# Half of the pair maxima go through PSUM, and the scores of two blocks lie contiguous there

## The chip, the core and the metric

The kernel runs on one core of a Trainium2 chip. The core has a matrix engine (TensorE, PE in the profile; its weight loads are the row PEld), a vector engine (VectorE, DVE), an activation engine (ScalarE, ACT), a general engine (GpSimd, POOL) and a queue that issues DMAs (SyncE, SP). Each has its own in-order stream of instructions, and they meet only at semaphores. PE writes to PSUM, which has 8 banks of 512 fp32 values per partition; POOL does not use PSUM in this kernel.

The metric is device time in microseconds (us). Three runs of the kernel before took 932.29, 934.55 and 936.86 us; the median is 934.55 us.

## What is computed

The inputs are q, k and v with 8 batches, 8 heads, 576 positions and 64 values per head, and two weight matrices of 512 x 2048 and 2048 x 512. All are fp32. Cut to what matters:

```python
scores = scale * np.matmul(q, k.transpose(0, 1, 3, 2))            # 576 x 576 for each of 64 heads
kth = np.partition(scores, -32, axis=-1)[..., -32:-31]            # the 32nd largest of a row
scores = np.where(scores >= kth, scores, -1e9)
attn = exp(scores - max) / (sum + 1e-9)
x = (attn @ v) as 4608 tokens x 512
h = x @ w_in;  out = np.maximum(h, 0) ** 2 @ w_out                # 4608 x 512
```

The costly step is the 32nd largest of 576 values in each of 36,864 rows.

## The kernel before

**The unit of work** is a task: two row blocks of 128 partitions with 576 scores each. In most tasks the two blocks are the same 128 query rows of two heads (a head pair), so that each head has its 64 values on its own half of the partitions of the transposed q and k (tile `qk`). In the others (`gi == Z`, 16 of 144) they are the last 64 rows of four heads, for two head pairs. There are 144 tasks.

**A task goes through these steps**, by the lines of the profile:

1. `scores` (L505 to L514) or `scores_z` (L516 to L524): PE writes the 2 x 576 fp32 scores to banks 0 to 2 (tile `ss` of pool `ps_s`, a single buffer). The first 512 columns of each block have a bank of their own, the two rests of 64 columns are next to each other in bank 2. The first head's matmuls use the array's rows 0 to 63, the second head's rows 64 to 127. All is one operation of the plan, one after the other on PE.
2. Two copies on ACT bring the scores to SBUF, tile `s`: L533 (1024 columns) and L535 (128 columns).
3. `m`, L589 on DVE: the maximum of each of 288 pairs of a row (column c with column c + 288), for both blocks; one operand is read from PSUM and the other from `s`.
4. `big`, L594 on DVE: the maximum of two pairs, 144 quad maxima per row, to the first quarter of tile `f`, a tensor_reduce.
5. POOL works out the other elements by sums and differences of bit patterns (L586): `t1` = both elements of a pair added, `t2` = both pair maxima added, `mid` = `t2` less `big`, `low` = `t1` less `m`. `f` then holds each row sorted into quad maxima, the lesser pair maxima and the lesser elements.
6. Three rounds on DVE take the largest eight of a prefix of `f` (MAX8, L609) and replace them there (MATCH_REPLACE8, L613); prefixes are 104, 124 and 272 columns long. A last MAX8 over all 576 gives `kth` (L616). The replacing instructions wait for `mid`, the last MAX8 for `low`.
7. ACT makes `w` from `s` and `kth` (L624, twice). PE (`flip`, L644) transposes `s` by nine matmuls and adds nine of `w`, ACT takes the exponential (`p`, L657), PE multiplies with v (`vb,p`), and the sums are divided out.
8. When a chunk of tokens is complete, `feed` runs the two matrix products of the second part (`xt,win` and `wo,g` in the profile), with the square on ACT or POOL.

**The order** is written out by a planner (`Plan.schedule`, L120) before the kernel runs. Every operation has an engine, an assumed duration, a priority (a due time `tg` = 12 + 6 n for task n, with an offset) and the tiles that it takes. The planner plays the five streams against each other by the assumed durations, and whenever an engine is free, it gives it the ready operation of the lowest due time. The outcome is one fixed stream per engine; on the chip an instruction that is late holds up all behind it. A tile is given out again once all operations that use it have ended. For the score operation the planner assumes 1.25 us.

Of the kernel before, what the change touches and what calls it, by code (L numbers as in the profile page):

```python
# [5 lines left out]
ALU = mybir.AluOpType  # L6
ACTF = mybir.ActivationFunctionType
AX = mybir.AxisListType
# [283 lines left out]
def bass_top_k_attn__then__act_relu_squared_kernel(  # L292
# [8 lines left out]
    NB, H, S, D = q.shape  # L301
    assert H == 8 and S == 576 and D == 64, (NB, H, S, D)
    HALF, QUART = S // 2, S // 4
    NHP = 4
    NPAIR = NB * NHP
    NBLK = 9
# [12 lines left out]
    T0 = 12.0  # L319
    LEAD = 20  # L320
    ME = 10
    MQ = 0
    MP = 3
    LAG = 20
    STEP = 3.2
    LATE = 1.5
# [39 lines left out]
    ps32 = nc.alloc_psum_tensor("ps", [P, 8, 512], FP32)  # L366
    ps16 = ps32[:, :, :].bitcast(BF16)

    ps_s, ps_e, psum = Pool("ps_s", 1), Pool("ps_e", 1), Pool("psum", 2)
    BASE = {"ps_s": 0, "ps_e": 3, "psum": 6}  # L370

    def tile(nm):
        return Tile(pools[nm])

    def at(t):
        return mem[t.pool.name][t.slot]
# [7 lines left out]
    def wide(t):  # L384

        b = BASE[t.pool.name]
        return ps32[:, b:b + 3, :].rearrange("p b c -> p (b c)")[:, 0:2 * S]

    em = Emitter(nc)
    act, vec, gp, pe = nc.scalar, nc.vector, nc.gpsimd, nc.tensor  # L390
# [3 lines left out]
    Z = 4  # L394
# [26 lines left out]
    def two(ap, step, n_):  # L421

        return bass.AP(ap.tensor, ap.offset, [ap.ap[0], [step, 2], [1, n_]])
# [9 lines left out]
    def build(full, weights, pl):  # L433
# [7 lines left out]
        def load_pair(b, hp, base):  # L441
            rq, rk, rv = tile("rq"), tile("rk"), tile("rv")

            def load(t, src, queue=nc.sync):
                def fn():
                    r = at(t)
                    res = [queue.dma_start(r[:, 0:4, h, :], src[b, 2 * hp + h, 0:512, :].rearrange(
                        "(tb p) d -> p tb d", p=P)) for h in range(2)]
                    res.append(queue.dma_start(
                        r[0:64, 4, :, :], src[b, 2 * hp:2 * hp + 2, 512:576, :].rearrange("h p d -> p h d")))  # L450
                    return res
                return fn

            def loadv():
                r = at(rv)
                res = [nc.sync.dma_start(r[:, 4 * h:4 * h + 4, :], v[b, 2 * hp + h, 0:512, :].rearrange(
                    "(tb p) d -> p tb d", p=P)) for h in range(2)]

                for h, low, e in ((0, 0, 8), (1, 64, 9), (1, 0, 10) if hp % 2 == 0 else (0, 64, 11)):
                    res.append(nc.sync.dma_start(r[low:low + 64, e, :], v[b, 2 * hp + h, 512:576, :]))  # L460
                return res

            pl.op("sp", 2.3, base - 80, load(rq, q), w=[rq], take=[rq], sem=slot_sem, ndma=3)
            via = "act" if not full and not state["pairs"] else None
            state["pairs"] += 1
            pl.op("sp", 2.3, base - 79.9, load(rk, k, nc.scalar if via else nc.sync), w=[rk], take=[rk], sem=slot_sem,
                  ndma=3, via=via)
            pl.op("sp", 2.3, base - 70, loadv, w=[rv], take=[rv], sem=slot_sem, ndma=5)
            qk, vb = tile("qk"), tile("vb")
            tq, tk, tx = Tile(psum), Tile(psum), Tile(psum)  # L470

            def t4(o, src):
# [12 lines left out]
            pl.op("pe", .48, base - 44.9, t4(tk, rk), r=[rk], w=[tk], take=[tk], order=[o_q])  # L485
            pl.op("pe", .3, base - 44.8, t5, r=[rq, rk], w=[tx], take=[tx], order=[o_q])
            pl.op("act", .6, base - 42.5, lambda: act.copy(at(qk)[:, 0, 0:512], bank(tq)), r=[tq], w=[qk])
            pl.op("act", .6, base - 42.4, lambda: act.copy(at(qk)[:, 1, 0:512], bank(tk)), r=[tk], w=[qk])  # L488
            pl.op("act", .3, base - 42.3, lambda: act.copy(
                at(qk)[:, :, 512:576], bank(tx)[:, 0:128].rearrange("p (a c) -> p a c", a=2)), r=[tx], w=[qk])  # L490
            pl.op("gp", .8, base + 5, lambda: gp.tensor_copy(at(vb)[:, :, 0:D], at(rv)[:, :, :]),
                  r=[rv], w=[vb], take=[vb])
            return qk, vb

        def top_k(gi, qks, tg):

            n = state["n"]
            state["n"] += 1
            ss, st = Tile(ps_s), tile("s")

            def scores():
                o = wide(ss)
                for h, to, c0, n_ in ((0, 1024, 512, 64), (0, 0, 0, 512), (1, 512, 0, 512), (1, 1088, 512, 64)):  # L505
                    x = at(qks[h])
                    if to == 1088:
                        pe.wait_ge(fence, fences[0])
                    ins = mm(o[:, to:to + n_], x[64 * h:64 * h + 64, 0, 128 * gi:128 * gi + 128],
                             x[64 * h:64 * h + 64, 1, c0:c0 + n_], to != 1088)  # L510
                    if to == 1024:
                        fences[0] += 1
                        ins.then_inc(fence, 1)
                return ins  # L514

            def scores_z():  # L516
                o = wide(ss)
                for i in range(2):
                    x = at(qks[i])
                    for to, c0, n_, first in ((1024 + 64 * i, 512, 64, i == 0), (512 * i, 0, 512, True)):  # L520
                        for h in range(2):
                            ins = mm(o[64 * h:64 * h + 64, to:to + n_], x[64 * h:64 * h + 64, 0, 512:576],
                                     x[64 * h:64 * h + 64, 1, c0:c0 + n_], first)
                return ins  # L524

            qu = sorted(set(qks), key=lambda t: t.num)
            pl.op("pe", 1.25 if gi != Z else 1.4, tg - LEAD, scores if gi != Z else scores_z, r=qu, w=[ss], take=[ss, st])


            def flat():  # L530
                return at(st)[:, :, :].rearrange("p i c -> p (i c)")

            cp = [pl.op("act", 1.1, tg - LEAD + 1, lambda: act.copy(  # L533
                two(flat(), 640, 512), two(wide(ss), 512, 512)), r=[ss], w=[st]),
                pl.op("act", .35, tg - LEAD + 1, lambda: act.copy(  # L535
                    flat()[:, 512:640], wide(ss)[:, 1024:1152]), r=[ss], w=[st])]

            dk = [0]

            def dve(dur, fn, dp=0, **kw):  # L540
                dk[0] += 1
                return pl.op("dve", dur, tg + .33 * dk[0] + dp, fn, **kw)
# [11 lines left out]
            f = tile("f")  # L554
            prev = [[], []]
            if full:
                a, sh = tile("a"), tile("sh")
                for rnd in range(4):
                    src = st if rnd == 0 else f
                    for i in range(2):  # L560
                        get = dict(r=[st]) if rnd == 0 else dict(hold=[f])
                        if rnd == 3:
# [4 lines left out]
                                       after=prev[i], take=[a] if rnd == 0 and i == 0 else [],  # L567
                                       w=[a] if rnd == 0 else [], **(
                                           get if rnd == 0 else dict(hold=[f, a])))]
# [11 lines left out]
            else:  # L581

                m, t1, t2 = tile("m"), tile("t1"), tile("t2")

                def whole(dur, prio, op, o, x, y, **kw):
                    return pl.op("gp", dur, prio, lambda: gp.tensor_tensor(  # L586
                        o().bitcast(I32), x().bitcast(I32), y().bitcast(I32), op), **kw)

                dve(.67, lambda: vec.tensor_tensor(  # L589
                    at(m)[:, :, :], two(wide(ss), 736, HALF), two(flat()[:, HALF:], HALF, HALF), ALU.max),  # L590
                    dp=-ME, r=[ss], hold=[st], after=cp, w=[m], take=[m])
                whole(1.38, tg, ALU.add, lambda: at(t1)[:, :, :], lambda: at(st)[:, :, 0:HALF],
                      lambda: at(st)[:, :, HALF:S], r=[st], w=[t1], take=[t1])
                big = dve(.67, lambda: vec.tensor_reduce(  # L594
                    at(f)[:, :, 0:QUART], at(m)[:, :, :].rearrange("p i (a c) -> p i c a", a=2), AX.X, ALU.max),
                    dp=-MQ, r=[m], w=[f], take=[f])
                whole(.77, tg - MP, ALU.add, lambda: at(t2)[:, :, :], lambda: at(m)[:, :, 0:QUART],
                      lambda: at(m)[:, :, QUART:HALF], r=[m], w=[t2], take=[t2])
                mid = whole(.77, tg - MP, ALU.subtract, lambda: at(f)[:, :, QUART:HALF], lambda: at(t2)[:, :, :],
# [1 line left out]
                low = whole(1.38, tg + 2, ALU.subtract, lambda: at(f)[:, :, HALF:S], lambda: at(t1)[:, :, :],  # L601
                            lambda: at(m)[:, :, :], r=[t1, m], w=[f])
# [373 lines left out]
```

## Time and profile before

| | |
|---|---|
| median of three runs | 934.55 us |
| the profiled execution | 930.32 us |
| its span, first to last instruction | 928.2 us |
| DVE busy | 864.2 us |
| PE busy | 810.1 us |
| POOL busy | 750.3 us |
| ACT busy | 742.8 us |
| mean granted clock of PE | 0.985 |

The profiled execution is 0.45% under the median of the runs; 2.1 us of it lie outside its span. Busy time is the union of an engine's instructions: two that overlap count once. Matmuls are pipelined, and each is shown until its result has left the array, so that the distance between the starts of two matmuls, not the duration of one, is the time that it takes from PE.

### The profile page before, as it was taken

Reading aid. Unit: us, or ns where it says so; the run is one execution under the profiler, and the core shown is the slowest. Engines: PE = TensorE matmul, PEld = TensorE weight load, DVE = VectorE, ACT = ScalarE, POOL = GpSimd, SP = SyncE. Lnnn points to the kernel's source line nnn. Section 1 sums busy time; section 2 is a strip of 40 time slices with the busy share of each in tenths; the row PEclk is TensorE's granted clock in tenths of the full one; section 3 lists DMA queues with packets and bytes.
Section 4 is the critical chain, followed back from the end, with each engine's and each line's share of the span. In section 5 each row is a group of like instructions: output and inputs, shape, how many; then the busy total and the mean of one; then the engine's idle time right before and its main releaser. Section 6 shows DMA issues by size and latency. Waiting matters only on the chain.

```text
span 928.2 us, 20946 instructions
## 1 busy us (share of the span) xinstructions
PE 810.1 (87%) x7253; PEld 565.7 (61%) x7330; DVE 864.2 (93%) x3269; ACT 742.8 (80%) x1277; POOL 750.3 (81%) x794
## 2 busy tenths in 40 slices
PE   5766889997689999888888898888998999999996
PEld 4555567766465666656566666656666655665664
DVE  3999999999999999999999999999999999998931
ACT  3665898987699878997799977998779789787762
POOL 6998988878777888777877887877899986899961
PEclk9898999999899999999999999999999999999999
DMA  6742521034101222111210131111211010000101
GB/s 138 190 129 91 141 54 53 14 88 91 39 6 37 53 51 63 27 29 49 58 45 16 40 89 37 41 39 39 52 38 26 13 37 13 24 13 1 43 27 38
DMA packets 126978, 48.11 MB, mean 52 GB/s; under 512 B 119184, under 2 KB 119184, under 8 KB 126864
## 3 DMA queue, kind: packets, MB, share of 16 engines
q1 hardware_dynamic: 125664, 46.39, 19.8%
q8 instruction: 59, 0.97, 0.4%
q14 instruction: 55, 0.45, 0.2%
q10 hardware_dynamic: 1200, 0.30, 0.2%
HBM read 37.22 MB, written 9.44 MB: 50 GB/s over the span
## 4 chain that ended last, share of the span: by engine, by line
DVE 45%; PE 35%; ACT 14%; issue 3%; DMA 1%; POOL 1%; SPq 0%; DVEq 0%
PE ps L428 27%; DVE f L613 13%; DVE kth L616 10%; DVE c L609 10%; PE ps L431 9%; DVE m L589 6%; DVE f L594 5%; ACT p L657 5%; ACT w L624 3%; ACT s L533 2%; ACT g L737 1%; ACT g L751 1%; DMA rq<-in_q_dram 1%; ACT xt L711 0%; ACT qk L488 0%
## 5 line engine op out<-in xcount | busy, mean ns | idle before, releaser
L613 DVE MATCH_REPLACE8 f<-c,f 128x104 f32<-128x104 f32 (+2 forms) x864 | 267.2, 317 | 0.4 <-issue 0.3
L609 DVE MAX8 c<-f 128x8 f32<-128x104 f32 (+2 forms) x864 | 243.7, 321 | 0.1
L428 PE MATMUL ps<-qk 64*128 64x64 f32 (+3 forms) x1280 | 213.9, 454 | 32.8 <-DVE m L589 31.6
L624 ACT ACTIVATE w<-s,kth 128x576 bf16<-128x576 f32 x288 | 222.3, 782 | 6.2 <-DVE kth L616 6.1
L586 POOL TENSOR_TENSOR t<-s 128x576 int32<-128x576 int32 x144 | 203.1, 1413 | 17.7 <-ACT s L535 17.6
L431 PE MATMUL ps<-ident,s 128*128 128x128 f32 x1296 | 200.2, 283 | 16.0 <-ACT w L624 15.4
L533 ACT COPY s<-ps 128x1024 f32<-128x1024 f32 x144 | 146.5, 1017 | 84.2 <-PE ps L428 83.8
L616 DVE MAX8 kth<-f 128x8 f32<-128x576 f32 x288 | 203.4, 748 | 1.6 <-POOL f L586 1.6
L586 POOL TENSOR_TENSOR f<-t,f 128x288 int32<-128x288 int32 x144 | 114.4, 795 | 110.8 <-DVE f L594 94.7
L586 POOL TENSOR_TENSOR f<-t,m 128x576 int32<-128x576 int32 x144 | 202.7, 1408 | 0.0
L428 PEld LDWEIGHTS ps<-qk 64*128 64x128 f32 (+1 forms) x1280 | 129.2, 180 | 110.2 <-DVE m L589 48.1
L657 ACT ACTIVATE p<-ps 128x1152 bf16<-128x1152 f32 x144 | 162.9, 1131 | 33.5 <-PE ps L428 32.6
L431 PEld LDWEIGHTS ps<-ident,s 128*128 128x128 f32 x1296 | 147.0, 143 | 50.1 <-ACT w L624 21.1
L428 PE MATMUL ps<-xt,win 128*128 128x512 bf16 (+3 forms) x674 | 126.8, 324 | 13.7 <-ACT g L737 7.4
L428 PE MATMUL ps<-wo,g 128*128 128x512 bf16 x529 | 134.2, 379 | 4.5 <-ACT xt L711 1.2
L589 DVE TENSOR_TENSOR m<-ps,s 128x576 f32<-128x576 f32 x144 | 107.5, 747 | 19.3 <-ACT s L535 16.9
L428 PE MATMUL ps<-steep_bf,w 128*128 128x128 bf16 x1296 | 121.4, 221 | 0.0
L586 POOL TENSOR_TENSOR t<-m 128x288 int32<-128x288 int32 x144 | 115.1, 799 | 0.0
L594 DVE TENSOR_REDUCE f<-m 128x288 f32<-128x576 f32 x144 | 106.7, 747 | 0.1
L737 ACT ACTIVATE g<-ps 128x512 bf16<-128x512 f32 (+1 forms) x152 | 87.2, 581 | 20.2 <-PE ps L428 19.7
L428 PEld LDWEIGHTS ps<-steep_bf,w 128*128 128x128 bf16 x1296 | 98.4, 99 | 3.6
L428 PEld LDWEIGHTS ps<-xt,win 128*128 128x128 bf16 x704 | 57.7, 98 | 51.8 <-ACT g L737 11.8
(57 smaller groups left out, 774.6 us busy)
## 6 DMA issues: line engine op xcount, KB each, us to landing
rq<-in_q_dram SPq DMA_DIRECT2D x64, 128.0 KB, 2.5
rv<-in_v_dram SPq DMA_DIRECT2D x64, 128.0 KB, 2.4
rk<-in_k_dram SPq DMA_DIRECT2D x62, 128.0 KB, 2.6
out_dram<-o SPq DMA_DIRECT2D x31, 256.0 KB, 2.1
g<-in_moe_w_in_dram SPq DMA_DIRECT2D x8, 512.0 KB, 4.7
g<-in_moe_w_out_dram SPq DMA_DIRECT2D x8, 512.0 KB, 3.9
rv<-in_v_dram SPq DMA_DIRECT2D x96, 16.0 KB, 2.2
out_dram<-o SPq DMA_DIRECT2D x10, 128.0 KB, 2.4
```

Source lines behind the costliest of these rows:

```text
L428: return pe.matmul(o, l, r, start=start, stop=stop, skip_group_check=True)
L431: return pe.matmul(o, i, ident, is_transpose=True, skip_group_check=True, **kw)
L533: cp = [pl.op("act", 1.1, tg - LEAD + 1, lambda: act.copy(two(flat(), 640, 512), two(wide(ss), 512, 512)), r=[ss], w=[st]), pl.op("act", . ...
L586: return pl.op("gp", dur, prio, lambda: gp.tensor_tensor(o().bitcast(I32), x().bitcast(I32), y().bitcast(I32), op), **kw)
L589: dve(.67, lambda: vec.tensor_tensor(at(m)[:, :, :], two(wide(ss), 736, HALF), two(flat()[:, HALF:], HALF, HALF), ALU.max), dp=-ME, r=[ss] ...
L594: big = dve(.67, lambda: vec.tensor_reduce(at(f)[:, :, 0:QUART], at(m)[:, :, :].rearrange("p i (a c) -> p i c a", a=2), AX.X, ALU.max), dp ...
L609: lambda i=i, t=t, c0=c0, c1=c1: vec.max(eighth(t, i), at(f)[:, i, c0:c1]),
L613: lambda i=i, t=t, c0=c0, c1=c1: vec.match_replace(at(f)[:, i, c0:c1], eighth(t, i), at(f)[:, i, c0:c1], NEG), hold=[f])]
L616: ks.append(chain(kth, i, prev[i] + [low], .665, lambda i=i: vec.max(eighth(kth, i), at(f)[:, i, :]), hold=[f]))
L624: pl.op("act", .77, tw + .8 * i, lambda i=i: act.activation(at(wt)[:, i, :], at(st)[:, i, :], ACTF.Relu, bias=kth[:, i, n:n + 1], scale=-1.0),
L657: pl.op("act", 1.15, tt + 1, lambda: act.activation(at(pt)[:, :, :].rearrange("p k q -> p (k q)"), wide(e), ACTF.Exp, scale=0.125), r=[e], ...
L737: return act.activation(at(g)[:, 0:kf * nt], bank(hh)[:, 0:kf * nt], ACTF.Relu)
```

## The change

Three things are changed together.

*Where the scores lie.* The 2 x 576 scores are now contiguous over banks 0 to 2 (1152 columns), and one ACT copy of 1152 columns takes the place of the two copies.

*Two score operations in place of one.* `scores(0)` makes the first head's block (64 + 512 columns, banks 0 and 1), `scores(1)` the second head's (128 + 448 columns, banks 2 and 1). For the Z tasks, `scores_z(0)` and `scores_z(1)` are divided by head pair. The second one writes to bank 2, whose columns 128 to 415 are a new single-buffer tile `sq` of pool `ps_q`, and it takes this tile; so it waits until the previous user is through with it. The planner is told 0.2 and 1.05 us for them (0.65 and 0.75 for Z).

*The pair maxima in two halves.* `m1` is the upper half of the pair maxima (2 x 144), which DVE now writes to PSUM (`sq`); `m0` is the lower half, which goes to SBUF tile `m` as before. A new ACT copy `mc` brings `m1` to its place in `m`, since POOL needs it there. `big` is now a tensor_tensor maximum of `m0` in SBUF with `m1` in PSUM, 2 x 144 outputs, and waits for `m0` and for `mc`. Its due time is 6 us earlier (`MQ` 0 to 6).

The order of the last 64 positions of the second head is rotated, so v is loaded with shifted rows (`64 * h`); number and size of the DMAs stay.

```diff
@@ pools
+    ps_s, ps_q, ps_e, psum = Pool("ps_s", 1), Pool("ps_q", 1), Pool("ps_e", 1), Pool("psum", 2)
+    BASE = {"ps_s": 0, "ps_q": 2, "ps_e": 3, "psum": 6}
-    MQ = 0
+    MQ = 6
+    MA = 12
+    M1 = 1
@@ top_k
-                for h, to, c0, n_ in ((0, 1024, 512, 64), (0, 0, 0, 512), (1, 512, 0, 512), (1, 1088, 512, 64)):
+            def scores(h):
+                o, x = wide(ss), at(qks[h])
+                for to, c0, n_ in ((512, 512, 64), (0, 0, 512)) if h == 0 else ((1024, 448, 128), (576, 0, 448)):
...
-            pl.op("pe", 1.25 if gi != Z else 1.4, tg - LEAD, scores if gi != Z else scores_z, r=qu, w=[ss], take=[ss, st])
+            fn = scores if gi != Z else scores_z
+            sc = pl.op("pe", .2 if gi != Z else .65, tg - LEAD, lambda: fn(0), r=[qks[0]], w=[ss], take=[ss, st])
+            sc = pl.op("pe", 1.05 if gi != Z else .75, tg - LEAD, lambda: fn(1), r=[qks[1]], w=[ss] + ([sq] if M1 else []),
+                       take=[sq] if M1 else [], after=[sc])
-            cp = [pl.op("act", 1.1, tg - LEAD + 1, lambda: act.copy(
-                two(flat(), 640, 512), two(wide(ss), 512, 512)), r=[ss], w=[st]),
-                pl.op("act", .35, tg - LEAD + 1, lambda: act.copy(
-                    flat()[:, 512:640], wide(ss)[:, 1024:1152]), r=[ss], w=[st])]
+            cp = [pl.op("act", 1.2, tg - LEAD + 1, lambda: act.copy(
+                at(st)[:, :, :].rearrange("p i c -> p (i c)"), wide(ss)), r=[ss], w=[st])]
...
-                dve(.67, lambda: vec.tensor_tensor(
-                    at(m)[:, :, :], two(wide(ss), 736, HALF), two(flat()[:, HALF:], HALF, HALF), ALU.max),
-                    dp=-ME, r=[ss], hold=[st], after=cp, w=[m], take=[m])
+                    m1 = dve(.36, lambda: vec.tensor_tensor(quarter(), *parts(QUART, QUART), ALU.max), dp=-ME,
+                             r=[ss], hold=[st, sq], after=cp)
+                    m0 = dve(.36, lambda: vec.tensor_tensor(at(m)[:, :, 0:QUART], *parts(0, QUART), ALU.max), dp=-ME,
+                             r=[ss], hold=[st], after=cp, w=[m], take=[m])
+                    mc = pl.op("act", .45, tg - MA, lambda: act.copy(at(m)[:, :, QUART:HALF], quarter()), hold=[sq],
+                               w=[m], after=[m1, m0])
+                    big = dve(.36, lambda: vec.tensor_tensor(
+                        at(f)[:, :, 0:QUART], at(m)[:, :, 0:QUART], quarter(), ALU.max), dp=-MQ,
+                        hold=[m, sq], after=[m0, mc], w=[f], take=[f])
...
-                big = dve(.67, lambda: vec.tensor_reduce(
-                    at(f)[:, :, 0:QUART], at(m)[:, :, :].rearrange("p i (a c) -> p i c a", a=2), AX.X, ALU.max),
-                    dp=-MQ, r=[m], w=[f], take=[f])
```

More of the change, by code (lines that the diff above doesn't have):

```diff
@@ L303, in bass_top_k_attn__then__act_relu_squared_kernel @@
     HALF, QUART = S // 2, S // 4
+    REST = (512, 0)
     NHP = 4
@@ L367, in bass_top_k_attn__then__act_relu_squared_kernel @@
     ps16 = ps32[:, :, :].bitcast(BF16)
-    ps_s, ps_e, psum = Pool("ps_s", 1), Pool("ps_e", 1), Pool("psum", 2)
-    BASE = {"ps_s": 0, "ps_e": 3, "psum": 6}
+    ps_s, ps_q, ps_e, psum = Pool("ps_s", 1), Pool("ps_q", 1), Pool("ps_e", 1), Pool("psum", 2)
+    BASE = {"ps_s": 0, "ps_q": 2, "ps_e": 3, "psum": 6}
     def tile(nm):
@@ L455, in loadv @@
                 r = at(rv)
-                res = [nc.sync.dma_start(r[:, 4 * h:4 * h + 4, :], v[b, 2 * hp + h, 0:512, :].rearrange(
+                res = [nc.sync.dma_start(r[:, 4 * h:4 * h + 4, :], v[b, 2 * hp + h, 64 * h:64 * h + 512, :].rearrange(
                     "(tb p) d -> p tb d", p=P)) for h in range(2)]
                 for h, low, e in ((0, 0, 8), (1, 64, 9), (1, 0, 10) if hp % 2 == 0 else (0, 64, 11)):
-                    res.append(nc.sync.dma_start(r[low:low + 64, e, :], v[b, 2 * hp + h, 512:576, :]))
+                    res.append(nc.sync.dma_start(r[low:low + 64, e, :], v[b, 2 * hp + h, REST[h]:REST[h] + 64, :]))
                 return res
@@ L498, in top_k @@
             state["n"] += 1
-            ss, st = Tile(ps_s), tile("s")
-            def scores():
-                o = wide(ss)
-                for h, to, c0, n_ in ((0, 1024, 512, 64), (0, 0, 0, 512), (1, 512, 0, 512), (1, 1088, 512, 64)):
-                    x = at(qks[h])
-                    if to == 1088:
+            ss, st, sq = Tile(ps_s), tile("s"), Tile(ps_q)
+            def scores(h):
+                o, x = wide(ss), at(qks[h])
+                for to, c0, n_ in ((512, 512, 64), (0, 0, 512)) if h == 0 else ((1024, 448, 128), (576, 0, 448)):
+                    if to == 576:
                         pe.wait_ge(fence, fences[0])
                     ins = mm(o[:, to:to + n_], x[64 * h:64 * h + 64, 0, 128 * gi:128 * gi + 128],
-                             x[64 * h:64 * h + 64, 1, c0:c0 + n_], to != 1088)
-                    if to == 1024:
+                             x[64 * h:64 * h + 64, 1, c0:c0 + n_], to != 576)
+                    if to == 512:
                         fences[0] += 1
@@ L514, in scores, with scores_z @@
                 return ins
[L516 to L521, printed above, removed]
+            def scores_z(i):
+                o, x = wide(ss), at(qks[i])
+                if i == 0:
+                    runs = [((512, 512, 64), (0, 0, 512)), ((512, 0, 64), (0, 64, 512))]
+                else:
+                    runs = [((1024, 384, 128), (576, 512, 64), (640, 0, 384)), ((1024, 448, 128), (576, 0, 448))]
+                for k_ in range(3):
+                    for h in range(2):
+                        if k_ < len(runs[h]):
+                            to, c0, n_ = runs[h][k_]
                             ins = mm(o[64 * h:64 * h + 64, to:to + n_], x[64 * h:64 * h + 64, 0, 512:576],
-                                     x[64 * h:64 * h + 64, 1, c0:c0 + n_], first)
+                                     x[64 * h:64 * h + 64, 1, c0:c0 + n_], not 576 <= to < 1024)
                 return ins
-            qu = sorted(set(qks), key=lambda t: t.num)
-            pl.op("pe", 1.25 if gi != Z else 1.4, tg - LEAD, scores if gi != Z else scores_z, r=qu, w=[ss], take=[ss, st])
-            def flat():
-                return at(st)[:, :, :].rearrange("p i c -> p (i c)")
-            cp = [pl.op("act", 1.1, tg - LEAD + 1, lambda: act.copy(
-                two(flat(), 640, 512), two(wide(ss), 512, 512)), r=[ss], w=[st]),
-                pl.op("act", .35, tg - LEAD + 1, lambda: act.copy(
-                    flat()[:, 512:640], wide(ss)[:, 1024:1152]), r=[ss], w=[st])]
+            fn = scores if gi != Z else scores_z
[4 more added lines that the diff above has]
+                at(st)[:, :, :].rearrange("p i c -> p (i c)"), wide(ss)), r=[ss], w=[st])]
             dk = [0]
@@ L587, in whole, with parts, quarter @@
                         o().bitcast(I32), x().bitcast(I32), y().bitcast(I32), op), **kw)
-                dve(.67, lambda: vec.tensor_tensor(
-                    at(m)[:, :, :], two(wide(ss), 736, HALF), two(flat()[:, HALF:], HALF, HALF), ALU.max),
-                    dp=-ME, r=[ss], hold=[st], after=cp, w=[m], take=[m])
+                def parts(a, n_):
+                    return two(wide(ss)[:, a:], S, n_), at(st)[:, :, HALF + a:HALF + a + n_]
+                def quarter():
+                    return two(ps32[:, 2, 128:416], QUART, QUART)
+                if M1:
+                    m1 = dve(.36, lambda: vec.tensor_tensor(quarter(), *parts(QUART, QUART), ALU.max), dp=-ME,
[7 more added lines that the diff above has]
+                        hold=[m, sq], after=[m0, mc], w=[f], take=[f])
+                else:
+                    dve(.67, lambda: vec.tensor_tensor(at(m)[:, :, :], *parts(0, HALF), ALU.max), dp=-ME,
+                        r=[ss], hold=[st], after=cp, w=[m], take=[m])
+                    big = dve(.67, lambda: vec.tensor_reduce(
+                        at(f)[:, :, 0:QUART], at(m)[:, :, :].rearrange("p i (a c) -> p i c a", a=2), AX.X, ALU.max),
+                        dp=-MQ, r=[m], w=[f], take=[f])
                 whole(1.38, tg, ALU.add, lambda: at(t1)[:, :, :], lambda: at(st)[:, :, 0:HALF],
                       lambda: at(st)[:, :, HALF:S], r=[st], w=[t1], take=[t1])
-                big = dve(.67, lambda: vec.tensor_reduce(
-                    at(f)[:, :, 0:QUART], at(m)[:, :, :].rearrange("p i (a c) -> p i c a", a=2), AX.X, ALU.max),
-                    dp=-MQ, r=[m], w=[f], take=[f])
                 whole(.77, tg - MP, ALU.add, lambda: at(t2)[:, :, :], lambda: at(m)[:, :, 0:QUART],
```

## The prediction

> **What bounds the kernel now.** I read the shares of busy time first, then the same by stage, then what DVE and PE wait for, then single rows of the timeline for prices. By stage (the windows view; span, busy time of each engine with its instructions, granted PE clock, DMA share, GB/s):
>
> ```profile
> 0.00:100.00 100.00, 66.89 (x532) 51.40 (x534) 82.63 (x311) 60.11 (x97) 85.63 (x112) 0.91 0.55 138
> 100.00:850.00 750.00, 674.51 (x6143) 470.37 (x6209) 740.59 (x2803) 639.84 (x1101) 615.31 (x627) 1.00 0.17 42
> 850.00:928.00 78.00, 68.74 (x581) 43.94 (x588) 40.99 (x157) 42.81 (x80) 49.32 (x57) 0.98 0.10 32
> ```
>
> The order is PE, PEld, DVE, ACT, POOL. From 100 to 850 us DVE is busy 740.6 of 750: it is the bound, at about 5.95 us per task. The last 78 us belong to PE. The waits of DVE in the middle stage are small, and those of PE are waits for DVE:
>
> ```profile
> DVE f L613 <- POOL f L586: 6.1, 7, 1.9
> DVE m L589 <- ACT s L535: 1.9, 4, 0.8
> ...
> PE ps L428 <- DVE m L589: 27.4, 43, 2.8
> ```
>
> DVE never waits long for scores: the loop from `m` by way of scores and copies to the next `m` has room. What the change touches is priced from these groups (busy us, mean ns of one) and these PE rows (start, length):
>
> ```profile
> L533 ACT COPY s<-ps 128x1024 f32<-128x1024 f32 x144 | 146.5, 1017 | 84.2 <-PE ps L428 83.8
> L535 ACT COPY s<-ps 128x128 f32<-128x128 f32 x144 | 40.7, 282 | 0.0
> L589 DVE TENSOR_TENSOR m<-ps,s 128x576 f32<-128x576 f32 x144 | 107.5, 747 | 19.3 <-ACT s L535 16.9 <-POOL f L586 2.0
> L594 DVE TENSOR_REDUCE f<-m 128x288 f32<-128x576 f32 x144 | 106.7, 747 | 0.1
> L609 DVE MAX8 c<-f 128x8 f32<-128x272 f32 x288 | 112.6, 431 | 0.0
> ```
> ```profile
> 505.56 0.59 PE L428 MATMUL ps<-xt,win 128*128 128x512 bf16 x2
> 506.09 1.34 PE L428 MATMUL ps<-qk 64*128 64x64 f32 x8
> 507.37 0.29 PE L431 MATMUL ps<-ident_bf,x 128*128 128x128 bf16 x2
> ...
> 511.02 2.17 PE L428 MATMUL ps<-qk 64*64 64x64 f32 x16 [0.15 <-DVE m L589]
> 513.12 0.36 PE L428 MATMUL ps<-vb,p 128*128 128x65 bf16 x6
> ```
>
> **How full PE really is.** Its busy time counts pipeline tails, so I take starts. A score operation holds PE from 506.09 to 507.37, 1.28 us (the median over all is 1.278). It starts 0.53 us after a pair of 512-column matmuls whose own steps are 0.216 each (0.59 less 0.379 for one, as a group has it), so the change from full-array to half-array matmuls costs 0.09 on the way in; between other kinds the trace has no such gap. By starts: scores 128 x 1.28 + 16 x 2.10 + 144 x 0.09 = 210 us; transposes of s and matmuls of w 1296 x (0.109 + 0.056) = 214; the second part 2 x 576 x 0.216 = 249; v 47, q and k 31, x 8. Sum 759 us, 82% of the span. The same steps on the matmuls that start from 100 to 850 us give 632 us, 84%. Where PE was fullest, in 150 to 200, 750 to 800 and 850 to 900 us, it reached 93, 95 and 92%.
>
> **The change part by part.**
>
> *DVE.* `m` and `big` go, three instructions of half the length come. Durations overlap, so I use starts again: in the timeline a 576-column instruction is followed after 0.66 us (600 ns at 0.96 columns per ns, and 65 ns). 288 columns then take 0.365. Per task 3 x 0.365 = 1.10 for 1.33: 0.23 us less, 33 us over 144 tasks. No row has DVE writing to PSUM; `m` (reads PSUM) and `big` (does not) are both 747 ns, so PSUM as a source costs nothing visible. The upper bound is no overlap at all, 0.45 each by the 272-column MAX8 (0.431): 1.35, no gain. I take 0.23, since every DVE pair without a wait shows the overlap; an end below it has nothing for it.
>
> The Trainium skill speaks against cutting here: "VectorE: DVE Perf Modes", in its section on the fixed extra latency of SBUF-source instructions, advises tiles of at least 512 elements, and gives (N + 151)/0.96 ns for an fp32 tensor_tensor. By that, an estimate, the saving would be 2 x 757 less 3 x 457 = 143 ns per task, 21 us in all. The 747 ns rows agree with the formula as a duration, but not as a distance between starts.
>
> *ACT.* Removed: 146.5 + 40.7 = 187.2 us. Added: one copy of 1152 columns, 1.12 us by the slope between 128 and 1024 columns (the exponential of 1152 takes 1.131), 162 us; and `mc`, 288 columns, about 0.40 between the copies of 260 (382 ns) and 512 (583 ns). That is 58 us, with 0.38 and 0.58 as ends. ACT goes from 743 to 776 us; in the middle stage from 640 to about 669 of 750. Not the bound. `mc` waits for DVE, and behind it in ACT's stream stand `p` and `w`.
>
> *PE.* The columns stay, but not their company. The 1.28 us hold only because the two heads use different rows of the array: each head alone is two passes of 512 at 0.425 and two short ones, and the passes of the heads run in pairs. In the changed streams the second half waits for the previous `big`, and the planner has filled the time between: of 128 normal tasks 112 have other matmuls between the halves, of 16 Z tasks 14. What a half costs alone is to be read from the Z row: it is two successive operations of 576 columns, all row groups alike, 511.02 to 513.12: 2.10 us, 1.05 each. Apart, each half has the change of shape to itself: 0.09 in, and about 0.10 out (the last 512-column pass of a Z task is followed after 0.520, against 0.425 inside). 2.10 + 0.19 - 1.28 = 1.01 us more; added up by single passes it is 0.92. I take 0.95. For a Z task only 0.19 is new. In the middle stage some 102 such tasks lie: 97 + 3 = 100 us more, 632 to 732 of the present 750 us: **98%**. DVE asks for 741 less 126 x 0.23 = 712. PE takes over as the bound.
>
> *Waits.* New: `scores(1)` on PE waits for `big`, and what stands behind it are the transposes, v products and second-part matmuls of a PE that has no time to lose; `big` on DVE waits for `mc`, with the next MAX8 behind it; between `m0` and `big` stand two MAX8 of 576 (1.33 us), which cover 0.40 plus one more ACT copy, not `p` (1.13) and `w` (0.78) together. Gone: `f` for POOL's `mid`, 6 us in the middle, as `big` now runs one task ahead; I leave these in PE's shadow. POOL's work and the DMAs stay the same; SP is asked for no more.
>
> *Sum.* PE at 94%, between the mean (93) and the best of its three fullest stretches: 732/0.94 = 779 us for the middle stage, 29 more. At the start DVE saves 3 us and PE loses about as much: 0. In the last stage, already PE's, three tasks' scores: +3. The profiled execution of 930.3 us becomes 962. The runs' median lies 4 us above that execution, so I predict 965.
>
> **The rivals.**
>
> *A, PE is the bound with the usual holes* (the sum): at 95 and 92% the middle takes 771 and 796, which gives 958 and 983; with a few us for the first stage, 950 to 985. Chance 0.60.
>
> *B, faster: DVE stays the bound.* It ends on the other side, if the halves apart cost what they cost together; then the 33 us are all gained and the run takes about 900. It decides at PE's need: below 712 us in the middle stage. That asks for under 0.75 us per split task and no holes at all, or for the second half to overlap with what is put between, of which I see nothing, as those matmuls use all rows. Even a full PE leaves 732. Chance 0.07, with 900 to 929.
>
> *C, it comes out even:* the planner's order happens to keep PE at 97 to 98%, which no stretch of 50 us reached. 930 to 939, chance 0.10.
>
> *D, the loop becomes the bound.* From `m0` on: half (1.15 with both changes), the matmuls between (mean 1.07 by starts, over 1.5 in three tasks of ten), half (1.15), copy 1.12, `m1` and `m0` 0.73, and some 0.5 of latencies: 5.7 us on average, 6.2 and more where much stands between; a queue on ACT comes on top. If this is paid in every second task with 1 us, the middle stage becomes 126 x 6.5 = 819 us: about 1007. The present DVE waits (1.9 us for the copy) say nothing against it, as the present loop is 2 us shorter. Chance 0.23, 985 to 1015.
>
> **How the numbers follow.** A and D together are 0.83 for slower; 0.5% of the time, 4.7 us, is about what a measurement can tell from no change. Faster is B, 0.07; the same is C, 0.10. The range leaves out B, nearly all of C and the end of D: 938 to 1002. The unknown price of PSUM writes (up to 33 us on DVE) fits in it: under A DVE has 779 less 712 us to spare in the middle stage.
>
> **What the profile after should show.** DVE busy about 833 us, its share down to 87%, with waits for the one copy of `s` where it had none; the time of `qk` matmuls up from 214 to over 300 us; PE busy at 95% or more in the middle; three DVE instructions of about 0.45 us; the copy at 1.12 and `mc` at 0.4. If DVE stays at 98% and PE has holes, B is right and my price of a split half is wrong. If PE has over 10% holes and DVE waits at `m1`, it is D. If the granted clock falls with a fuller PE, all is later than I say.

## The result, and the profile after

The changed kernel takes 1032.6 us (four runs, 1026.8 to 1037.2) against 933.4 us for the kernel before beside it. The ratio is 1.106, with a 95% interval from 1.099 to 1.112: 10.6% slower, where 3.3% had been forecast and the range ended at 1002 us. The profiled execution took 1032.64 us with a span of 1030.8.

By stage (windows view of the changed kernel; span, busy time of PE, PEld, DVE, ACT, POOL, granted PE clock, DMA share, GB/s):

```profile
0.00:100.00 100.00, 85.10 (x469) 52.43 (x470) 69.03 (x279) 56.24 (x84) 73.66 (x100) 0.91 0.46 114
100.00:850.00 750.00, 728.28 (x5653) 442.56 (x5650) 663.04 (x2708) 611.56 (x985) 570.50 (x574) 0.99 0.18 44
850.00:950.00 100.00, 99.42 (x672) 53.98 (x672) 68.45 (x276) 75.60 (x131) 63.14 (x69) 1.00 0.05 15
950.00:1031.00 81.00, 71.53 (x575) 43.00 (x573) 38.60 (x152) 42.89 (x78) 47.29 (x54) 0.98 0.10 31
```

From 100 to 850 us PE is now busy 728 of 750, and DVE, which had 741, has 663. The page's chain of work that ended last says the same; in the kernel before, DVE held 45% of it and PE 35%:

```profile
PE 82%; ACT 8%; DVE 7%; issue 2%; POOL 1%; DMA 0%; SPq 0%
```

The granted clock of PE explains little of the loss: it is 0.980 on average against 0.985, which is some 5 us of the span (an estimate).

DVE's waits turn to the copy of the scores (engine, line, whom it waited for, us in total, times, longest):

```profile
DVE ps L601 <- ACT s L538: 124.0, 109, 14.9
DVE rzall L706 <- ACT av L704: 22.1, 7, 10.4
DVE f L607 <- ACT m L605: 16.7, 32, 3.5
```

PE itself hardly waits for the maxima: 14 us in all for `big` (L607) and `m0` (L603), where in the kernel before it waited 31.6 us for `m`.

```profile
PE ps L431 <- DVE f L607: 8.4, 12, 1.2
PE ps L431 <- DVE m L603: 5.8, 15, 1.0
```

The groups show that the new instructions cost about what was said: three DVE instructions of 0.44 to 0.47 us, one copy of 1.12 us, `mc` of 0.40 us.

```profile
L538 ACT COPY s<-ps 128x1152 f32<-128x1152 f32 x144 | 161.2, 1120 | 76.0 <-PE ps L431 72.1 <-PE ps L434 1.9
L601 DVE TENSOR_TENSOR ps<-ps,s 128x288 f32<-128x288 f32 x144 | 66.9, 465 | 125.4 <-ACT s L538 124.0
L607 DVE TENSOR_TENSOR f<-m,ps 128x288 f32<-128x288 f32 x144 | 63.6, 442 | 17.2 <-ACT m L605 16.7
L605 ACT COPY m<-ps 128x288 f32<-128x288 f32 x144 | 58.2, 404 | 6.8 <-DVE m L603 6.7
```

What was dearer than forecast is the split score operation. These are PE's rows around one task in the timeline (start, length):

```profile
505.33 1.35 PE L431 MATMUL ps<-qk 64*128 64x64 f32 x4
506.61 0.66 PE L434 MATMUL ps<-ident,rk 128*128 128x128 f32 x4
507.10 1.03 PE L431 MATMUL ps<-wo,g 128*128 128x512 bf16 x4
508.06 1.24 PE L431 MATMUL ps<-qk 64*128 64x128 f32 x4
509.23 0.81 PE L431 MATMUL ps<-vb,p 128*128 128x65 bf16 x20
```

The first half holds PE from 505.33 to 506.61 (1.28 us), the second from 508.06 to 509.23 (1.17 us), each with 0.09 us before it for the change of shape: 2.63 us, against 1.28 + 0.09 before. Added up by starts, scores take 376 us of PE instead of 210 (the prediction's sum). All of PE's work by starts is about 928 us, more than the 839 us that DVE is busy. Apart from the scores it is unchanged.

Two theories were tested. **S**: the price of the split on PE sets the time. **L**: the new wait of the second half for `big`, through the shared bank 2, makes the loop from task to task too long, and PE is busy only because it is late.

### The profile page after: what moved, and what is told of

The parts are those of the page before. It is cut to its first block, busy times and chain, and to the rows that moved or that the text cites. A ratio compares the mean times of both kernels' runs of the same rounds, so it can differ in the third digit from the quotient of the medians.

```text
span 1030.8 us, 21271 instructions
## 1 busy us (share of the span) xinstructions
PE 984.3 (95%) x7362; PEld 592.0 (57%) x7362; DVE 839.1 (81%) x3413; ACT 786.3 (76%) x1277; POOL 754.6 (73%) x794
## 4 chain that ended last, share of the span: by engine, by line
PE 82%; ACT 8%; DVE 7%; issue 2%; POOL 1%; DMA 0%; SPq 0%
PE ps L431 64%; PE ps L434 18%; ACT s L538 3%; DVE f L634 2%; ACT p L678 2%; DVE c L630 1%; DVE kth L637 1%; ACT w L645 1%; DVE m L603 1%; DVE ps L601 1%; ACT g L758 1%; DVE f L607 0%; POOL t L589 0%; DMA rq<-in_q_dram 0%; ACT xt L732 0%
## 5 line engine op out<-in xcount | busy, mean ns | idle before, releaser
L431 PE MATMUL ps<-qk 64*128 64x64 f32 (+8 forms) x1312 | 384.3, 445 | 16.6 <-DVE f L607 8.4
L538 ACT COPY s<-ps 128x1152 f32<-128x1152 f32 x144 | 161.2, 1120 | 76.0 <-PE ps L431 72.1
L637 DVE MAX8 kth<-f 128x8 f32<-128x576 f32 x288 | 205.5, 747 | 1.9 <-POOL f L589 1.9
L434 PE MATMUL ps<-ident,s 128*128 128x128 f32 x1296 | 203.9, 286 | 3.2 <-ACT w L645 1.9
L431 PEld LDWEIGHTS ps<-qk 64*128 64x128 f32 (+1 forms) x1312 | 150.9, 180 | 89.8 <-DVE f L634 23.0
L601 DVE TENSOR_TENSOR ps<-ps,s 128x288 f32<-128x288 f32 x144 | 66.9, 465 | 125.4 <-ACT s L538 124.0
L431 PE MATMUL ps<-wo,g 128*128 128x512 bf16 x576 | 144.3, 380 | 0.4 <-ACT g L758 0.4
L431 PE MATMUL ps<-xt,win 128*128 128x512 bf16 (+3 forms) x704 | 133.8, 328 | 7.5 <-ACT g L758 3.0
L431 PEld LDWEIGHTS ps<-wo,g 128*128 128x128 bf16 x576 | 49.7, 98 | 66.5 <-issue 17.9
```

What stands on the lines that cost most here:

```text
L431: return pe.matmul(o, l, r, start=start, stop=stop, skip_group_check=True)
L434: return pe.matmul(o, i, ident, is_transpose=True, skip_group_check=True, **kw)
L538: cp = [pl.op("act", 1.2, tg - LEAD + 1, lambda: act.copy(at(st)[:, :, :].rearrange("p i c -> p (i c)"), wide(ss)), r=[ss], w=[st])]
L601: m1 = dve(.36, lambda: vec.tensor_tensor(quarter(), *parts(QUART, QUART), ALU.max), dp=-ME, r=[ss], hold=[st, sq], after=cp)
L637: ks.append(chain(kth, i, prev[i] + [low], .665, lambda i=i: vec.max(eighth(kth, i), at(f)[:, i, :]), hold=[f]))
```

## The experiments

**1. The scores joined again, everything else as changed.**

```diff
-            sc = pl.op("pe", .2 ..., lambda: fn(0), ..., take=[ss, st])
-            sc = pl.op("pe", 1.05 ..., lambda: fn(1), ..., take=[sq], after=[sc])
+            pl.op("pe", 1.25 if gi != Z else 1.4, tg - LEAD, lambda: [fn(0), fn(1)][1], r=qu,
+                  w=[ss, sq], take=[ss, st, sq])
```

> Edit: the changed kernel, with both halves of the scores in one PE operation again (so they run side by side in the array); it takes the quarter of bank 2 as a whole, so all scores of a task now wait for the previous `big`. Everything else as changed. Theory S (a split half is dear on PE: in the trace after, 1.28 and 1.17 us and twice 0.09 for the change of shape, 2.63 us against 1.37 before, for all 128 normal tasks): score time on PE falls from 376 us (by starts) to about 220, PE is no longer full, and DVE with its 33 us less becomes the bound again: 895 to 930 us. Rival L (the new wait for `big` and the longer loop cost the time): the wait now holds back the whole score operation, so the loop is longer still: 1000 us or more, DVE waiting for the copy of `s` in most tasks.

941.9 us, ratio to the kernel before 1.010 (1.008 to 1.013). So 91 of the 99 us went with the split, though all scores now wait for `big`. S has its main point, L's 1000 us are out. The expected 895 to 930 were missed too: DVE has 709 us of work in the middle stage, and waits. One score operation in this layout takes 1.44 us (median), not 1.28.

```profile
DVE ps L601 <- ACT s L538: 32.7, 36, 12.6
DVE f L634 <- POOL f L589: 20.2, 19, 2.4
...
DVE f L607 <- ACT m L605: 12.3, 15, 2.5
```

**2. The kernel before, with the two heads one after the other.**

```diff
-                    if to == 1088:
+                    if to in (512, 1088):
                         pe.wait_ge(fence, fences[0])
...
-                    if to == 1024:
+                    if to in (1024, 0):
                         fences[0] += 1
                         ins.then_inc(fence, 1)
```

> Edit: the kernel before, with one thing added: inside the score operation the second head's matmuls wait until the first head's have ended. Streams, layout, maxima and planner are as before. Theory S: the two halves one after the other take 2.58 us where they took 1.28 side by side (so the trace after shows it where they stand together): 128 x 1.3 = 166 us more for PE, 917 of need; PE about 94% full in the middle stage: 631 + 110 x 1.3 = 774, over 0.94 gives 823 us there, 990 to 1025 in all, PE busy 95%, DVE with waits for the copy of `s`. Rival L (wait for `big`, bank 2, loop): none of it is here, and DVE has its old work: 930 to 950 us.

1112.5 us, ratio 1.193: more than S said. The score operation takes 2.63 us (median) where it took 1.28, and nothing else was touched:

```profile
500.04 2.69 PE L428 MATMUL ps<-qk 64*128 64x64 f32 x8
502.66 0.66 PE L431 MATMUL ps<-ident,s 128*128 128x128 f32 x4
```

The direction is S's, and the 930 to 950 us that L gave for the old maxima are out. But here the whole 2.63 us also stand between `m` and the copy, and DVE waited 138 us for the copy; so this run is a price of lost company and of a longer loop together. PE's granted clock was low as well (0.94 on average, down to 0.5 in a stretch near 100 us), so part of the excess may be that.

**3. `big` from SBUF alone, in the kernel before.** It asks whether the way through PSUM is needed.

```diff
-                big = dve(.67, lambda: vec.tensor_reduce(
-                    at(f)[:, :, 0:QUART], at(m)[:, :, :].rearrange("p i (a c) -> p i c a", a=2), AX.X, ALU.max),
+                big = dve(.36, lambda: vec.tensor_tensor(
+                    at(f)[:, :, 0:QUART], at(m)[:, :, 0:QUART], at(m)[:, :, QUART:HALF], ALU.max),
```

> Edit: the kernel before, with one line changed: `big` is a tensor_tensor maximum of the two halves of `m`, both in SBUF (2 x 144 outputs), in place of the tensor_reduce over 2 x 288. No PSUM, no split. If an SBUF source costs DVE no more than a PSUM source: 0.365 for 0.66 us by starts, 144 x 0.30 = 43 us less on DVE, the bound; with PE at 751 us of need, 885 to 905 us. If two SBUF operands get in the way of POOL, or the other way round (the reason there might be for the way through PSUM): `big` or POOL's instructions get longer, over 0.5 us for `big` or over 0.83 for POOL's 288-column ones, and the time is 920 us or more.

939.3 us, ratio 1.005 (1.001 to 1.008). The second alternative came true: with both operands in SBUF the same maximum takes 631 ns, with one in PSUM 442 (L607 above). DVE's busy time falls by 17 us and not by 43.

```profile
L594 DVE TENSOR_TENSOR f<-m 128x288 f32<-128x288 f32 x144 | 89.0, 631 | 0.2
```

POOL's instructions are hardly longer (0.82 us for 0.795 in the 288-column `mid`). The mean of 631 ns hides two cases, which the trace tells apart. 90 of the 144 maxima take under 0.49 us, and 84 of these start while POOL runs nothing. The other 54 take 0.53 to 1.7 us: every one starts while a POOL instruction runs, and ends 0.31 us after that instruction has ended. In the changed kernel, with one operand in PSUM, 97 of the 144 start while POOL runs, and none takes more than 0.46 us. So with both operands in SBUF the maximum waits for POOL's instruction to end. One of the 54:

```profile
434.72 1.40 POOL L586 TENSOR_TENSOR f<-t,m 128x576 int32<-128x576 int32 x1
434.81 1.62 DVE L594 TENSOR_TENSOR f<-m 128x288 f32<-128x288 f32 x1
```

**4. The layout alone**: scores joined, `m` and `big` as before (`M1 = 0`, `MQ = 0`), so that only the contiguous scores and the one copy are left.

> Edit: the changed kernel with both halves of the scores in one operation and with the maxima as before (`m` whole, in SBUF, `big` a tensor_reduce, due time of `big` as before). What is left of the change is the contiguous scores and the one copy. Theory S: PE and DVE have the work of the kernel before, ACT 26 us less, which is not the bound: 925 to 938 us. Rival L has nothing to add, as nothing waits for `big`: the same. If it is over 950, the layout itself (a bank that both heads write) costs PE time, and neither theory is whole.

943.9 us, ratio 1.010 (1.006 to 1.015). The layout costs 1% by itself, a little over the expected interval: its score operation takes 1.44 us. In the old order one head begins with its long matmuls and the other with its short one; in the new one both begin with the short ones. There the kernel has the second head's 448 columns wait for the first head's short matmuls (both write to bank 1): in the trace of experiment 1 they start 0.26 us after the matmul of the same head before them, against 0.11 in a half alone. That is 0.15 of the 0.16 us. Between experiments 4 and 1 the maxima through PSUM change nothing in the time.

**5. PE spared elsewhere**: the changed kernel without the mask matmuls.

```diff
-                for o, c, start in outs:
-                    ins = mm(o, wf[:, c:c + 128], minus[:, :], False)
```

> Edit: the changed kernel without the nine matmuls of `w` in every task (the mask is left out, so that all keys count in the softmax); everything waits for `w` as it did. PE is spared 1296 x 0.056 = 73 us. Theory S (PE, full with 928 us of need by starts, sets the time): the time falls by about as much, 950 to 970 us. Rival L (the loop from `big` over the scores to the next `big` sets it, PE being busy only because it is late): the loop is as long as before, 1015 us or more.

1014.7 us, 18 us less, at the edge of what L expected (1015 or more) and far from S's. By progress (the end of `kth` of a task in the trace), tasks 48 to 128 take 6.23 us each, against 6.58 in the changed kernel: 0.35 of the 0.50 us spared. But the 16th task ended at 142 us instead of 129. The granted clock was 0.80 in the first 100 us and 0.87 in the next 200; a second execution had a mean clock of 0.966 for 0.946 and took as long. PE's waits for `big` and `m0` are 15.5 us in all here, so the loop does not account for the missing time either. The clock may account for part of it (106 us at half clock against 37 in the changed kernel, about 34 us of PE's time, an estimate), but the second execution speaks against its being all. This run left the question open.

**6. `big` ahead of `mc`**, in the joined kernel of experiment 1: the loop without the two MAX8 of 576.

```diff
-                    big = dve(.36, ..., dp=-MQ, hold=[m, sq], after=[m0, mc], w=[f], take=[f])
+                    big = dve(.36, ..., dp=-ME, hold=[m, sq], after=[m1, m0], w=[f], take=[f])
-                    mc = pl.op("act", .45, ..., hold=[sq], w=[m], after=[m1, m0])
+                    mc = pl.op("act", .45, ..., hold=[sq], w=[m], after=[big])
```

> Edit: the run with the joined scores (942 us, DVE 832 us busy but waiting for the copy of `s`, for `mc` and for POOL), with `big` ahead of `mc`: it follows `m0` at once and waits for nothing on ACT, and `mc` waits for `big`. The loop from one score operation to the next loses the two MAX8 of 576 between `m0` and `big` (1.33 us) and gains `mc` (0.4 and a queue on ACT). If the loop is what kept the joined run from the 33 us that DVE was spared: 905 to 930 us. If it is the longer score operation (1.44 for 1.28 us) and PE's queue: 938 to 945, as before.

945.7 us, ratio 1.015 (1.009 to 1.022): no gain. PE now waits for `mc` (33 us) in place of `big` (35 us).

**7. The same maxima in the old layout**, with `big` ahead of `mc` and the two copies kept.

> Edit: the kernel before, with its layout, its two copies and its one score operation (1.28 us), and only the maxima changed: `m1` to PSUM (bank 2, columns 128 to 415), `m0`, `big` at once after them, then `mc`. Against the run with the same order in the contiguous layout it spares PE 0.16 us per normal task (20 us in all) and costs ACT 26 us. DVE is spared 30 us. If DVE's work counts: 895 to 920. If one engine less full does not help since the loop is longer by the wait for `mc`: 930 or more.

938.8 us, ratio 1.006 (1.002 to 1.011). DVE is busy 828 us for 864, and a task takes 5.88 us in the steady part for 5.99; the last task ends 12 us earlier than before. The end after it takes 44 us for 29.

**8. True durations for the planner**, in the changed kernel: 1.3 and 1.2 us for the halves.

```diff
-            sc = pl.op("pe", .2 if gi != Z else .65, ...
-            sc = pl.op("pe", 1.05 if gi != Z else .75, ...
+            sc = pl.op("pe", 1.3 if gi != Z else 1.15, ...
+            sc = pl.op("pe", 1.2 if gi != Z else 1.15, ...
```

> Edit: the changed kernel with the durations that the halves had on the chip told to the planner (1.3 and 1.2 us for 0.2 and 1.05; 1.15 each for Z): only the order of the streams changes, no work. If PE's need alone sets the time: 1020 to 1045, as the changed kernel. If the wrong durations put PE's work in an order that makes it and the others wait: 20 us less or more, 1010 and below.

1009.3 us, ratio 1.082 (1.072 to 1.093). The work is the same and PE's need by starts is 928 us in both, but 23 us are gained by the order. The clock has a small part in that at most: the second run, with a mean clock of 0.985, took 1012.9 us, and two runs of the changed kernel with 0.982 and 0.987 took 1032.5 and 1037.2. In the steady stage PE has almost no idle time left:

```profile
300.00:850.00 550.00, 547.33 (x4174) 326.94 (x4172) 489.43 (x1996) 464.66 (x748) 417.12 (x420) 1.00 0.15 38
```

The changed kernel has 536.18 of 550 there.

**9 to 12. Is the gain held back by the due times?** Three runs with due times spaced 5.75 us instead of 6.0 (`PER`), and one that in addition gives `mc` a due time 8 us earlier (`MA` 12 to 20).

> Edit: the run with the old layout, the joined scores and the maxima through PSUM with `big` ahead of `mc` (939 us), with the spacing of the due times 5.75 for 6.0 us per task. In that run a task took 5.88 us in the steady part (before: 5.99), and the last task was through at 887 us (before: 899), but the end after it took 44 us for 29: matrix products of the second part, which the planner holds back to due times counted at 6.0 us per task, were left over. If that is where the gain went: the end takes about 30 us again, 905 to 925 us. If PE's total need or the loop sets the end: 930 or more.

> Edit: the changed kernel with joined scores (942 us) and the spacing of the due times 5.75 for 6.0. There a task took 5.92 us in the steady part, but the last 16 tasks 126 us (before: 113) and the end 29 us. If the due times held work back to the end: 915 to 930. If the longer score operation (1.44 us) on a PE that is full near the end is the cause: 935 to 945.

> Edit: the kernel before with the spacing of the due times 5.75 for 6.0, nothing else: the control for the two others. DVE sets the pace there, at 5.99 us per task, so due times of 5.75 can only shift the second part ahead: 925 to 940 us, no gain over 1%. If it gains as much as the others do, the spacing is the gain and not the maxima.

> Edit: as the run with the old layout and spacing 5.75, with the due time of `mc` 8 us earlier, so that on ACT it goes ahead of whatever else is ready. PE waited 46 us for `mc` in the run with spacing 6.0, as all scores of the next task wait for it. If this wait costs time: 5 to 15 us less than its neighbour with spacing 5.75. If it is covered: within 3 us of it.

The old layout with PSUM maxima took 935.4 us (ratio 1.002, 0.998 to 1.006), the joined changed kernel 939.1 (1.005, 1.002 to 1.009), the kernel before 935.1 (1.001, 0.997 to 1.004). So the idea was wrong: the end in the first of them is 44 us as it was. With the earlier `mc` the old layout takes 928.4 us, ratio 0.992 (0.989 to 0.996): the only fp32 version of the full computation that beats the kernel before, by 0.8%, and 7 us below its neighbour, within what was expected of the wait. Its steady tasks take 5.81 us. What keeps the end at 44 us was not found.

**13 and 14. Only the price of a score matmul changed**: transposed q and k kept in bf16, in the changed kernel and in the kernel before as a control.

```diff
-        "qk": ([P, 2, S], FP32, 5),
+        "qk": ([P, 2, S], BF16, 5),
```

> Edit: the changed kernel with transposed q and k kept in bf16 (the scores then have bf16 precision); the same planner input, so the same order of the streams, the same split, the same wait of the second half for `big`, the same loop. Only the price of a half on PE changes: one pass for two, and shorter: about 0.5 us for 1.2, PE's need about 730 us for 928. Theory S: with PE out of the way the time falls by 90 us or more, to 905 to 940, within 2% of the control beside it. Rival L: the waits are all there, and the time stays 4% or more over the control.

> Edit: the kernel before with transposed q and k in bf16, the control. PE is spared about 100 us, but DVE sets the pace, with unchanged work: 918 to 935 us by both theories.

918.8 us against 922.6 for the control (four runs each on one chip; 0.985 and 0.989 of the fp32 kernel before, intervals 0.978 to 0.992 and 0.981 to 0.996). A half now holds PE for about 0.35 us. The split, its order and the wait for `big` are all there, and the change costs nothing against its control, as S says. By itself this does not exclude a loop that is long because two halves lie in it: each is 0.8 to 0.9 us shorter here, and in experiment 1 that loop is shorter too. Against such a loop stand PE's waits in the changed kernel, 14 us in all for `big` and `m0`. The page of the changed kernel in bf16 and its DVE waits:

```profile
PE 765.9 (84%) x6627; PEld 495.7 (54%) x6706; DVE 827.5 (90%) x3413; ACT 772.7 (84%) x1277; POOL 753.2 (82%) x794
```
```profile
DVE ps L601 <- ACT s L538: 21.2, 18, 11.3
```

The wait for the copy falls from 124 to 21 us, of which 11 is the start. In the steady part a task takes 5.77 us, against 5.97 in the control: here most of the DVE saving that was forecast (0.23 us per task) can be seen. The last 16 tasks give most of it back: they take 123 us against 110 in the control.

## Why the prediction was right and wrong

*Right: who becomes the bound, and why.* PE takes over from DVE, since a head's matmuls lose their company in the array. The profile after shows PE with 928 us of work by starts and with hardly a wait for DVE; experiments 1 and 13 show it by two routes, joining the halves and making them cheap.

*Right: how full PE gets.* 94% was taken from three stretches; in the changed kernel PE's need by starts is 795 of the 850 us from 100 to 950, 93.6%. There is luck in the match: with the same work in another order, experiment 8, it is about 97%, the share that rival C named.

*Right: the terms of DVE and ACT.* The copy of 1.12 and `mc` of 0.40 us came out; DVE's busy time is 839 us, 833 had been said. PSUM as a target costs DVE 465 for 446 ns. Against the Trainium skill's formula that the prediction cites ("VectorE: DVE Perf Modes", 457 ns for 288 columns), durations fit; for the distance between starts the timeline has `m1` to `m0` at 0.37 us (504.03 to 504.40), as predicted.

*Wrong: the price of a half, the term "2.10 + 0.19 - 1.28 = 1.01, I take 0.95".* It measures 1.26 us (2.63 less 1.37). The Z row was the wrong neighbour: its matmuls are 64 x 64, whose weight loads take 0.137 us, while those of a normal task are 64 x 128, 0.191. Alone in its rows, a pass of 64 columns is followed after 0.160 us and one of 512 after 0.485; in the Z row it was about 0.10 and 0.43. The trace before held these distances inside the joined operation: the first head's matmuls come 0.160, 0.111 and 0.485 us apart there too, so that this head by itself takes the 1.28 us of the whole. I read only the total. That the weight loads make the difference fits the shapes, but was not isolated. The Trainium skill has a sentence that points that way: "TensorE: Matmul & The Clock Gate", in its part on packing small matmuls, says that weight loads overlap with running matmuls only when their row group differs. The rows here agree with it in part only: the matmuls of `w` use all rows of the array and have a load of 0.099 us each, and still follow one another after 0.056 us.

*Wrong: the count, "of 128 normal tasks 112".* All 128 pay. The second half has a dependency on the first, and the emitted stream has PE wait for its own semaphore there, so that even halves that stand side by side run one after the other; the shortest of the 16 such pairs takes 2.58 us in the changed kernel, and experiment 2 shows the price of such a wait, 2.63 us. The wait was in the order of the streams, and I had looked only at what stood between.

Together the scores take about 165 us more (128 x 1.26 = 161 in the normal tasks, the rest in the Z tasks), not about 109 (112 x 0.95 and 16 x 0.19). With 1.26 us for all tasks the prediction's own sum gives (632 + 110 x 1.26 + 3)/0.94 = 823 us for the middle stage, and 930 + 73 + 3 = 1006 us in all.

*Left out: the planner's error.* I noted that it was told 0.2 and 1.05 us, and put no price on it. Experiment 8 gives 23 us, most of the remaining 26.

*Rivals.* B (faster), C (even) did not come. D (the loop) is not the cause: its sign was over 10% holes in PE, and PE has 6% by starts and waits 14 us in all for the maxima that close the loop. But the loop is not free. In the joined versions DVE has 30 us less to do and the time does not fall, with waits for the copy, for POOL and for `mc`; none of the 33 us showed in the whole time of an fp32 version without tuning the due time of `mc`, and with it 5 us did.

## What to carry to other kernels

Before an operation is split, ask what runs beside it inside its engine: two streams of matmuls on different rows of the array may together take no longer than one of them alone (1.28 us here), and a dependency between them, or anything put between them, doubles the time. Price a part alone by rows of its own shape, taken from inside the joint operation if need be, and look for waits of an engine on itself in the new stream. An order written by a planner is only as good as its durations: give it measured ones whenever an operation changes its shape.

## What the runs showed of the hardware

A maximum of 2 x 144 fp32 values on DVE took 631 ns on average with both operands in SBUF and 442 with one of them in PSUM. With both in SBUF it took about 0.44 us where POOL ran nothing; in the 54 cases over 0.5 us it ended 0.31 us after the POOL instruction that ran at its start (experiment 3).

Two matmul streams on the two halves of the array's rows, in one operation, took 1.28 us, 1.44 where the second had to wait within it for the first one's short matmuls, and 2.63 one after the other.

PE's granted clock fell to between 0.5 and 0.7 for some 100 us near the start in experiments 2 and 5, dipped likewise in both bf16 runs (mean 0.94 in each), and stayed at 0.99 or more in every stage of the profiled run of experiment 8, where PE was busy 97% of the span (92% and 95% in experiments 2 and 5). A PE that stands idle is not the reason everywhere: in experiment 5 the clock was 0.50 for 41 us in which PE was busy 40.65, and the transposes of `s` followed one another after 0.213 us there, 0.109 at the full clock. What sets it off was not found.

```profile
59.00:100.00 41.00, 40.65 (x163) 24.48 (x164) 31.29 (x127) 22.67 (x32) 31.47 (x32) 0.50 0.29 92
```
